# Head of an attention and feed-forward kernel: score tiles cut across pairs, masks of four pairs on TensorE, first up weights in two parts

## The chip, the cores and the metric

The kernel runs on one core of one Trainium2 chip. The metric is the device time of one launch in microseconds (us); where several runs are shown it is their median. The engines are TensorE (PE in the profile, with its weight loads as PEld), ScalarE (ACT), VectorE (DVE), GpSimd (POOL) and SyncE (SP, which here only issues DMAs).

## What is computed

Inputs are q, k, v of 8 sequences, 8 heads, 576 positions and 64 features, 16 further "beacon" keys and values a head that every query may see, and two weights w_in (512 x 2048) and w_out (2048 x 512), all in float32.

```
scores = (q @ concat(beacon_k, k).T) / sqrt(64)       # 576 x 592
scores = where(causal, -1e9, scores)                  # the 16 beacon columns are never masked
a      = softmax(scores)
x      = (a @ concat(beacon_v, v))  -> 4608 tokens x 512
h      = x @ w_in
out    = maximum(0.01 * h, h) @ w_out                 # 4608 x 512
```

## The kernel before

Work goes by pairs of heads: a sequence has four pairs, so there are 32, numbered 0 to 31. For a pair the kernel computes the transposed scores: the 592 keys are cut in five blocks of up to 128, and of each block only the queries that may see it are computed. A score matmul contracts over 64 features, so the two heads of a pair use the upper and the lower 64 rows of TensorE and run side by side, each into a PSUM bank of its own. ScalarE turns a tile of scores into exponentials (scale 0.125) in a bf16 buffer aT, of which there are four. On the diagonal a triangle has to become zero: `triangle` (L287 to L297) does it with a GpSimd affine select on aT, after the exp. `value` (L374) multiplies aT, as weights, with V and a column of ones, whose result is the softmax's denominator; VectorE takes its reciprocal (L388) and scales (L389) into x_nat, and `x_transposes` (L400) turns x_nat into columns of xT on TensorE, with a copy on VectorE or ScalarE (L410).

The feed-forward part works on chunks of 512 tokens. An up (`moe1`, L431) is four 512-column matmuls with w_in (L442) and a leaky relu on ScalarE into gT (L450); there are 16 in a chunk. A down uses gT and w_out: for the first chunk 16 steps of four 512-column matmuls (`moe2_plain`, L507, with its matmul at L512), for the later ones steps of eight 256-column matmuls (L537) that combine sums of operands.

All five engines run their instructions in the order in which the code records them. The first eight pairs (two sequences) are the head, whose order is written out by hand as strings of steps, played by `run` (L692, the strings at L751 to L770): l loads q or k of a pair (L158, issued by GpSimd), V a part of v (L209, L214), i and o a half of w_in (L131) and w_out (L137), q and k turn a loaded operand on TensorE (`t_q`, L231, nine or eighteen small transposes, and a copy at L249), s is a score tile with its exp, m some masks, v half of a pair's values, x its turn into xT, u an up, d a down, w some matmuls on a blank tile whose result nobody reads (`unused`, L653), and W the same in a bank that the next values use (L665). A pair of the head has four score tiles of its own (`score` L256, table SCORES at L50), of 512, 464, 416 and 288 columns in each bank. From pair 8 on, events with due times (L796 to L835) interleave the work, and the scores are cut otherwise: the 1664 columns of a pair lie one after the other (FLAT, L66), pair after pair, and `stretch` (L299) cuts them in tiles of 512, so that a tile may hold the end of one pair and the beginning of the next. Between those events `fill` puts ups and downs on TensorE.

A tile of the framework's pool waits, when it is taken again, for the readers of its last use: score tiles have two such places, all other PSUM tiles of one bank share four. GpSimd's DMAs use eight semaphores in turn, so a DMA is issued only when the one eight before it has landed.

Of the kernel before, what the change touches and what calls it, by code (L numbers as in the profile page):

```python
# [15 lines left out]
def kernel(  # L16
# [33 lines left out]
    SCORES = [  # L50
        [(0, 0, 512, 0)],
        [(1, 112, 464, 512)],
        [(2, 240, 336, 976), (0, 496, 80, 1312)],
        [(3, 368, 208, 1440), (4, 496, 80, 1648)],
    ]
    ACOLS = 1776
    PADS = (1392, 1728)
    BASE = [0, 512, 976, 1440, 1648]
# [3 lines left out]
    LAID = 2 * NPAIR  # L62
    TURNED = 8
    NR = 96

    FLAT = [0, 576, 1040, 1376, 1584, 1664]  # L66

    def acol(g, c, q0):
        if g >= LAID:
            return FLAT[c] + q0 - OFF[c]  # L70
        if c == 0:
            return 1312 if q0 == 496 else q0
        if c == 4:
            return 1648
        return BASE[c] + q0 - OFF[c]

# [12 lines left out]
    blank = singles.tile([128, 128], BF16, name="blank")  # L89
    w_in_sb = [singles.tile([128, NJ, DF // 2], BF16, name=f"w_in_sb{i}") for i in range(2)]  # L90
# [12 lines left out]
    a_bufs = [singles.tile([128, 2, ACOLS], BF16, name=f"aT{i}") for i in range(NA)]  # L103
# [13 lines left out]
    def make_pads():  # L117
        nc.vector.memset(k_all[:, :, NB + S :], 0.0)
        for t in a_bufs:
            for c in PADS:  # L120
                nc.vector.memset(t[:, :, c : c + 48], 0.0)
# [7 lines left out]
    def load_w_in(i):  # L129
        n = DF // 2  # L130
        loaded["w_in", i] = nc.gpsimd.dma_start(  # L131
            out=w_in_sb[i], in_=w_in_r[:, :, i * n : (i + 1) * n]
        )
# [122 lines left out]
    def score(g, n):  # L256
        qT, kT = qk[g]
        if n == 0:
            probs[g] = a_bufs[g % NA]
        aT = probs[g]  # L260
        parts = SCORES[n]
        sc = ps_sc.tile([128, 2, 512], FP32, name="sc", tag="sc")
        c0 = parts[0][3]
        for c, q0, w, col in parts:
            for par in range(2):
                ps_ = slice(par * 64, par * 64 + 64)
                nc.tensor.matmul(  # L267
                    out=sc[:, par, col - c0 : col - c0 + w],
                    lhsT=kT[ps_, c * 128 : (c + 1) * 128],
                    rhs=qT[ps_, q0 : q0 + w],  # L270
# [11 lines left out]
    def mask(g, part):  # L282
        aT = probs[g]
        for lo, n, rows in MASKS[part]:
            triangle(aT, lo, n, rows)
# [582 lines left out]
```

## Time and profile before

| | |
|---|---|
| time, median of 3 runs | 326.24 us (324.75 to 326.97) |
| the profiled execution | 325.23 us, its span 323.5 us, clock of TensorE 0.999 |
| busy: PE, PEld, DVE, ACT, POOL | 98%, 66%, 45%, 62%, 57% of the span |
| score matmuls of the head (L267) into exp (L276) | 32 exps, 25.9 us, 875 ns each on average |
| masks (L289), whole kernel | 160 selects, 59.7 us, 404 ns on average |
| ups (L442) | 640 matmuls, 135.7 us busy |
| w_in's halves: issue to landing | 13.1 + 11.4 us and 19.5 + 11.9 us |

Times in the profile count from the start of the span. Each row of a timeline gives the start, the length, engine and line, the operation, the output and the inputs, the shape, the number of instructions merged in the row, and in brackets how long the engine sat idle before and what ended that. A matmul's length includes the way through the array; the spacing of starts tells what it costs in a row of others.

### The profile page before, as it was taken

What the parts mean: (1) busy time and instruction counts of PE and PEld (TensorE: products, weight loads), DVE (VectorE), ACT (ScalarE), POOL (GpSimd) and SP (SyncE); (2) the same over time, 40 slices, a digit from 0 to 9 for tenths busy, and PEclk for the clock granted to TensorE, in tenths of its full rate; (3) what the DMA queues carried; (4) which work ended last, traced back from release to release, by engine and by line L of the source; (5) the groups of instructions that cost most, each with busy time, mean ns of one, the idle gap of its engine ahead of it and who ended that gap; (6) DMA issues with size and microseconds to landing.
All of it is one profiled execution on the core that took longest, in us unless ns stands there. A gap on an engine that the chain in (4) does not pass through costs nothing.

```text
span 323.5 us, 8521 instructions
## 1 busy us (share of the span) xinstructions
PE 317.3 (98%) x3429; PEld 213.4 (66%) x3429; DVE 146.1 (45%) x297; ACT 199.3 (62%) x336; POOL 184.7 (57%) x354
## 2 busy tenths in 40 slices
PE   8999999999999999999999999999999999999995
PEld 5574565445687558845888888656865785466684
DVE  3473354518446145434552455345444542325444
ACT  4969862487765786478647873786468415653420
POOL 8895968999997687659875977664221000000000
PEclk9999999999999999999999999999999999999999
DMA  8999999999999999999999999999112112000203
GB/s 140 137 206 175 147 214 120 188 165 190 157 138 169 218 147 107 124 174 80 154 192 160 110 127 115 196 128 135 52 53 79 24 54 97 2 1 32 79 20 132
DMA packets 155928, 39.93 MB, mean 123 GB/s; under 512 B 143040, under 2 KB 153152, under 8 KB 155888
## 3 DMA queue, kind: packets, MB, share of 16 engines
q0 software_dynamic: 99824, 18.54, 91.3%
q1 hardware_dynamic: 55792, 20.77, 37.1%
q8 instruction: 27, 0.44, 0.6%
q14 instruction: 13, 0.11, 0.1%
q10 hardware_dynamic: 272, 0.07, 0.1%
HBM read 37.22 MB, written 9.44 MB: 144 GB/s over the span
## 4 chain that ended last, share of the span: by engine, by line
PE 77%; DMA 10%; POOL 5%; ACT 3%; DVE 2%; issue 2%; DVEq 0%; POOLq 0%; ACTq 0%
PE acc L442 31%; PE acc L537 30%; PE av L359 6%; PE sc L314 6%; DMA w_out_sb<-in_moe_w_out_dram 4%; PE acc L512 4%; DMA w_in_sb<-in_moe_w_in_dram 4%; POOL aT L289 2%; DMA gsum<-in_k_dram 2%; ACT aT L333 2%; POOL gsum L158 2%; ACT aT L329 1%; DVE p L565 0%; ACT gT L450 0%; DVE u L565 0%
## 5 line engine op out<-in xcount | busy, mean ns | idle before, releaser
L442 PE MATMUL acc<-xT,w_in_sb 128*128 128x512 bf16 (+1 forms) x640 | 135.7, 358 | 0.3 <-ACT aT L329 0.3
L450 ACT ACTIVATE gT<-acc 128x512 bf16<-128x512 f32 x144 | 82.8, 621 | 46.4 <-PE acc L442 46.2
L442 PEld LDWEIGHTS <-w_in_sb 128*128 128x128 bf16 x640 | 59.6, 98 | 52.4 <-issue 2.9
L289 POOL TENSOR_SCALAR_AFFINE_SELECT aT<-aT 128x256 bf16<-128x256 bf16 (+2 forms) x160 | 59.7, 404 | 51.7 <-ACT aT L329 30.9
L537 PEld LDWEIGHTS <-gT 128*128 128x128 bf16 x512 | 48.8, 98 | 9.1 <-issue 1.8
L333 ACT ACTIVATE aT<-sc 128x1024 bf16<-128x1024 f32 (+3 forms) x64 | 51.8, 895 | 0.0
L537 PE MATMUL acc<-w_out_sb,gT 128*128 128x256 bf16 x384 | 46.2, 273 | 0.4 <-ACT gT L450 0.4
L329 ACT ACTIVATE aT<-sc 128x512 bf16<-128x512 f32 (+3 forms) x64 | 29.0, 522 | 27.9 <-PE sc L314 27.7
L388 DVE RECIPROCAL rec<-av 128x6 f32<-128x6 f32 (+1 forms) x64 | 12.0, 188 | 67.0 <-PE av L359 66.3
L359 PEld LDWEIGHTS <-aT 128*128 128x128 bf16 (+1 forms) x960 | 36.7, 98 | 8.3 <-issue 0.6
L537 PEld LDWEIGHTS <-gsum 128*128 128x128 bf16 x384 | 36.5, 98 | 6.2 <-issue 0.4
L359 PE MATMUL av<-v_aug,aT 128*128 128x65 bf16 (+1 forms) x960 | 39.4, 194 | 0.3 <-ACT gT L450 0.2
L214 POOL DMA_DIRECT2D v_aug<-in_v_dram x40 | 34.2, 859 | 4.1 <-DMA w_in_sb<-in_moe_w_in_dram 3.4
L568 ACT COPY p<-acc 128x512 f32<-128x512 f32 (+1 forms) x25 | 14.5, 580 | 35.6 <-PE acc L537 35.6
L171 POOL DMA_DIRECT2D k_nat<-in_k_dram x48 | 34.9, 733 | 1.3 <-DMA w_out_sb<-in_moe_w_out_dram 0.6
L171 POOL DMA_DIRECT2D q_nat<-in_q_dram x48 | 34.8, 731 | 0.6 <-issue 0.3
L389 DVE TENSOR_TENSOR x_nat<-av,rec 128x384 bf16<-128x384 f32 (+1 forms) x64 | 31.4, 491 | 2.2
L537 PE MATMUL acc<-w_sum,gsum 128*128 128x256 bf16 x256 | 31.9, 273 | 0.0
L276 ACT ACTIVATE aT<-sc 128x1024 bf16<-128x1024 f32 (+3 forms) x32 | 25.9, 875 | 3.5 <-PE sc L267 3.5
L620 DVE TENSOR_TENSOR gsum<-gT 128x1024 bf16<-128x1024 bf16 x16 | 11.0, 688 | 28.1 <-ACT gT L450 28.1
L314 PE MATMUL sc<-qT,kT 64*128 64x80 bf16 (+22 forms) x384 | 22.0, 250 | 0.3
L314 PEld LDWEIGHTS <-kT 64*128 64x128 bf16 x384 | 12.9, 94 | 10.9 <-issue 7.6
(62 smaller groups left out, 227.3 us busy)
## 6 DMA issues: line engine op xcount, KB each, us to landing
out_dram<-p SPq DMA_DIRECT2D x26, 256.0 KB, 3.2
q_nat<-in_q_dram POOLq DMA_DIRECT2D x48, 72.0 KB, 5.5
k_nat<-in_k_dram POOLq DMA_DIRECT2D x48, 72.0 KB, 5.0
v_aug<-in_v_dram POOLq DMA_DIRECT2D x24, 128.0 KB, 6.1
w_in_sb<-in_moe_w_in_dram POOLq DMA_DIRECT2D x2, 1024.0 KB, 11.7
w_out_sb<-in_moe_w_out_dram POOLq DMA_DIRECT2D x2, 1024.0 KB, 11.7
out_dram<-u SPq DMA_DIRECT2D x8, 256.0 KB, 2.7
gsum<-in_q_dram POOLq DMA_DIRECT2D x8, 144.0 KB, 6.9
```

What stands on the lines that cost most here:

```text
L171: nc.gpsimd.dma_start(out=t[:, :, par], in_=(q, k)[which][b, 2 * hp + par].rearrange("(t p) d -> p t d", p=NR),)
L214: nc.gpsimd.dma_start(out=dst[lo : ROWS[c], c, :, 0:D], in_=v[b, :, OFF[c] : OFF[c] + n].rearrange("h p d -> p h d"),)
L276: nc.scalar.activation(out=aT[:, :, c0 : c0 + w], in_=sc[:, :, 0:w], func=AF.Exp, scale=0.125)
L289: nc.gpsimd.affine_select(out=view, in_=view, compare_op=ALU.is_ge, fill=0.0, base=128 - n if lo == 0 else 0, channel_multiplier=-1, patte ...
L314: nc.tensor.matmul(out=(sc[par] if apart else sc[:, par])[:, at : at + b - a], lhsT=kT[ps_, c * 128 : (c + 1) * 128], rhs=qT[ps_, q0 : q0 ...
L329: nc.scalar.activation(out=probs[g][:, par, lo:hi], in_=sc[par][:, at : at + hi - lo], func=AF.Exp, scale=0.125)
L333: nc.scalar.activation(out=probs[g][:, :, lo:hi], in_=sc[:, :, at : at + hi - lo], func=AF.Exp, scale=0.125)
L359: nc.tensor.matmul(out=avv[:, n, 0 : D + 1], lhsT=aT[0 : ROWS[c], par, a0 : a0 + 128], rhs=va[0 : ROWS[c], c, 2 * hp + par, :], start=(c = ...
L389: nc.vector.tensor_tensor(out=x_nat[:, t0:t1].rearrange("p t e d -> p (t e) d"), in0=avv[:, :, 0:D], in1=rec[:, n0:n1, None].to_broadcast( ...
L442: nc.tensor.matmul(out=acc[:, lo:hi], lhsT=w_in_cols(fc, j), rhs=xT[:, j, x0 : x0 + hi - lo], start=(j == 0), stop=(j == NJ - 1), skip_gro ...
L450: nc.scalar.activation(out=gT[i][:, fc, :], in_=acc, func=AF.Prelu, alpha=0.01)
L537: nc.tensor.matmul(out=acc[:, lo : lo + HD], lhsT=left(i, n, fc, tile), rhs=right(n, fc), start=(lo == 0 and fc == 0), stop=(fc == HF - 1) ...
```

## The change

The head now uses the dense cut too. `score`, `mask`, their tables and the second layout of aT are gone; step s takes a tile number from 0 to 25 and calls `stretch`, for the eight pairs' 8 x 1664 columns. For tiles 0 to 12 (pairs 0 to 3) `stretch` is called with `hidden`: after the scores of a tile, `hide` adds a matmul for each piece of a diagonal triangle and each of the two banks, with the identity as weights and a bias tile (0 or -32768, made once by GpSimd) as the moving operand; only the first score matmul of a bank starts it, and the rest add or write. The exp then gives zeros, and those tiles have no masks on GpSimd. Tiles 13 to 25 keep the selects. The first half of w_in is loaded in two parts, both issued before pair 4's q and k; pair 3's q and k are issued before the first V parts; all of pair 5's, pair 6's and most of the second V buffer's loads are recorded ahead of the first matmul. The steps of the head are put in a new order with other numbers of unused matmuls; the first three ups come before pair 4 is turned. The unused steps e and W are gone, and the reciprocals have four buffers instead of two.

```diff
-    def load_w_in(i):
-        n = DF // 2
-        loaded["w_in", i] = nc.gpsimd.dma_start(
-            out=w_in_sb[i], in_=w_in_r[:, :, i * n : (i + 1) * n]
+    def load_w_in(i, part=0, parts=1):
+        n, w = DF // 2, DF // 2 // parts
+        nc.gpsimd.dma_start(
+            out=w_in_sb[i][:, :, part * w : (part + 1) * w],
+            in_=w_in_r[:, :, i * n + part * w : i * n + (part + 1) * w],
         )
...
+    def make_bias():
+        nc.gpsimd.affine_select(
+            out=bias,
+            in_=blank,
+            compare_op=ALU.is_ge,
+            fill=-32768.0,
+            base=0,
+            channel_multiplier=-1,
+            pattern=[[1, 128]],
+        )
...
+    def hide(out, lo):
+        nc.tensor.matmul(
+            out=out,
+            lhsT=ident,
+            rhs=bias[:, lo : lo + out.shape[1]],
+            start=False,
+            stop=True,
+            skip_group_check=True,
+        )
+
-    def stretch(parts, apart=False):
+    def stretch(parts, apart=False, hidden=False):
...
-                        start=True,
+                        start=not hidden or at == 0,
                         stop=True,
                         skip_group_check=True,
                     )
+                end = min(b, FLAT[c] + QT[c][1])
+                if a < end:
+                    hides.append((at, end - a, a - FLAT[c] + (NB if c == 0 else 0)))
                 at += b - a
+        if hidden:
+            for at, n, first in hides:
+                for par in range(2):
+                    hide(bank(par)[:, at : at + n], first)
...
             if op == "s":
-                score(*a)
+                stretch(tile_parts(0, a[0]), hidden=a[0] < 13)
             elif op == "m":
-                mask(*a)
+                triangles(tile_parts(0, a[0]))
...
-        run("l1.1 l2.0 l2.1 V0.0 V0.1 l3.0 l3.1 V0.2 V0.3 V0.4 l4.0 l4.1 i0")
+        make_bias()
+        run("l1.1 l2.0 l2.1 l3.0 l3.1 V0.0 V0.1 V0.2 V0.3 V0.4 i0.0.2 i0.1.2 l4.0 l4.1 l5.0 l5.1 i1 l6.0 l6.1 V1.0 V1.1 V1.2 V1.3")
...
-        unused(13)
+        unused(18)
...
-        run("q0.1 k0 w2.384 s0.0 m0.0 w3.256 s0.1 q1 s0.2 m0.1 k1 s0.3 m0.2")
-        run("w2.384 s1.0 m1.0 q2 s1.1 k2 w2.384 s1.2 m1.1 w2.384 s1.3 m1.2 W0.0.4 s2.0 m2.0 W0.0.4 s2.1 W0.0.6 q3 l5.0 l5.1 s2.2 k3 w4.384 v0.0 m2.1 s2.3 i1 m2.2 W0.1.4 s3.0 m3.0 v1.0 s3.1 v0.1 s3.2 v1.1 m3.1 l6.0 l6.1 s3.3 x0.1 m3.2")
-        run("v2.0 V1.0 V1.1 q4 v2.1 x1 k4.1 v3.0 v3.1 x2.1 s4.0 s4.1 x3 m4.0 V1.2 V1.3 V1.4 l7.0 l7.1 u u s4.2 s4.3 q5 k5 m4.1 m4.2 u o0 u")
+        run("q0.1 k0 w3.384 s0 w1.384 q1 s1 k1 w1.384 s2 q2 s3 k2 w1.384 s4 q3 w1.384 s5 k3 w2.384 s6 w2.384 s7 w2.384 s8 w1.384 v0.0 s9 v1.0 s10 v0.1 s11 v1.1 v2.0 s12 x0 v2.1 x1.1 v3.0 v3.1 x2.1 w3.384 x3.1")
+        run("u u u q4 u k4.1 u s13 m13 V1.4 u s14 l7.0 l7.1 m14 q5 u k5 s15 m15 u s16 m16 o0 u s17 m17 u")
         load_beacon_k(2, B, nc.gpsimd)
-        run("s5.0 s5.1 m5.0 u u u s5.2 s5.3 q6 k6 m5.1 m5.2 o1 u u s6.0 s6.1 m6.0 u v4.0 u v4.1 y4 N8.0 N8.1 u s6.2 s6.3 q7 k7 m6.1 m6.2 u")
+        run("q6 s18 m18 u k6 u s19 m19 o1 u s20 m20 u s21 m21 q7 u k7 v4.0 s22 m22 u N8.0 N8.1 v4.1 y4")
...
-        run("u v5.0 u v5.1 N9.0 s7.0 s7.1 m7.0 d x5 v6.0 v6.1 T8 d s7.2 s7.3")
+        run("s23 m23 v5.0 s24 m24 N9.0 v5.1 s25 m25 v6.0 d x5 v6.1 d T8")
...
-        run("m7.1 m7.2 N9.1 u b8.2 b9.2 b10.2 b11.2 x6 v7.0 T9 v7.1 d d d N10.0 N10.1 d V2.0 V2.1 x7 t0 T10")
+        run("v7.0 N9.1 d b8.2 b9.2 b10.2 b11.2 x6 v7.1 T9 d d d N10.0 N10.1 d V2.0 V2.1 x7 t0 T10 d d d d")
```

## The prediction, made before the result was known

> **What bounds the kernel now.** I read the page first: busy shares, then the 40 slices. TensorE (PE) is busy 98% of the span and 9 tenths in every slice but the two ends, with its full clock granted.
>
> ```profile
> span 323.5 us, 8521 instructions
> PE 317.3 (98%) x3429; PEld 213.4 (66%) x3429; DVE 146.1 (45%) x297; ACT 199.3 (62%) x336; POOL 184.7 (57%) x354
> PE   8999999999999999999999999999999999999995
> ```
>
> So the question for any edit is how much it adds to or takes from what TensorE issues, and which of its waits it ends. The table of stretches (columns: stretch, length, busy time of PE, PEld, DVE, ACT, POOL, then clock and DMA) says that after the head (from 76.9 us) there is almost nothing left to win by waiting less:
>
> ```profile
> 5.60:25.20 19.60, 19.27 (x398) 12.69 (x396) 11.99 (x27) 15.23 (x21) 18.45 (x38) 1.00 1.70 174
> 76.90:200.00 123.10, 122.74 (x1405) 89.84 (x1404) 56.85 (x118) 85.15 (x151) 96.80 (x182) 1.00 1.75 147
> ```
>
> The first stretch looks as full but is not all work: it holds warm-up matmuls (L657, L669). Next the timeline of TensorE at a place where warm-ups (L657, 128 rows) and score matmuls (L267, 64 rows, two at a time) alternate:
>
> ```profile
> 11.58 0.50 PE L657 MATMUL av<-blank 128*128 128x384 bf16 x2
> 12.01 0.35 PE L267 MATMUL sc<-qT,kT 64*128 64x336 bf16 x4
> 12.29 0.50 PE L657 MATMUL av<-blank 128*128 128x384 bf16 x2
> 12.73 0.30 PE L267 MATMUL sc<-qT,kT 64*128 64x208 bf16 x4
> ```
>
> Two 384-column matmuls stream for 2 x 0.163 = 0.33 us (the group of four at 15.73 takes 0.82, its last matmul 0.33: 0.163 apart), yet the scores start 0.43 and 0.44 us after them: 0.10 us is lost at the change of row shape. Then what ends the head's first part, on ScalarE, GpSimd and TensorE:
>
> ```profile
> 17.20 3.89 ACT L276 ACTIVATE aT<-sc 128x576 bf16<-128x576 f32 x5 [0.84 <-PE sc L267]
> ...
> 20.24 1.73 POOL L289 TENSOR_SCALAR_AFFINE_SELECT aT<-aT 128x256 bf16<-128x256 bf16 x5
> 21.93 0.59 POOL L158 DMA_DIRECT2D gsum<-in_q_dram  x1
> 22.51 0.61 POOL L158 DMA_DIRECT2D gsum<-in_k_dram  x1
> 23.12 0.70 POOL L289 TENSOR_SCALAR_AFFINE_SELECT aT<-aT 128x256 bf16<-128x256 bf16 x2
> ...
> 22.78 1.49 PE L359 MATMUL av<-v_aug,aT 128*128 128x65 bf16 x30
> 24.11 0.42 PE L405 MATMUL tp<-ident,x_nat 112*128 112x112 bf16 x5
> 24.46 0.59 PE L267 MATMUL sc<-qT,kT 64*128 64x512 bf16 x4
> 24.98 0.43 PE L405 MATMUL tp<-ident,x_nat 112*128 112x112 bf16 x5
> 25.25 1.52 PE L442 MATMUL acc<-xT,w_in_sb 128*128 128x512 bf16 x6
> ...
> 52.24 3.61 PE L512 MATMUL acc<-w_out_sb,gT 128*128 128x512 bf16 x16 [0.34 <-DMA w_out_sb<-in_moe_w_out_dram]
> ```
>
> The last exp of pair 3 ends at 21.09 (17.20 + 3.89), its last two masks wait behind two DMA issues until 23.82, pair 3's value matmuls take 1.33 us instead of the 0.95 of an undisturbed x30, and the first up matmul (L442) starts at 25.25. Later one wait of the head, for the second half of w_out at 52.2, shows on TensorE.
>
> **What the Trainium skill says.** TensorEngine Tiling (Array Packing), Key Properties: "Mode switching requires drain". The 0.10 us above is that; the trace agrees and prices it. TensorE: Matmul & The Clock Gate, "Wait — 56ns, not 53.3ns?": warm matmuls of 128 columns start 55.6 ns apart. The trace agrees: the five transposes from 24.98 to 25.25 move 576 columns in 0.27 us. The same page, "Architectural detail": GpSimd's queue is in order, so masks wait behind DMA issues, as at 21.93. PSUM — Partial Sum Buffer, The four PSUM rules: a matmul without the first flag adds where an earlier one wrote since the bank was cleared, and overwrites elsewhere. So the mask matmuls need no help from another engine; nothing in this trace shows such an addition at these tiles.
>
> **The change, part by part.**
> Mask matmuls: a pair's triangles are 112 + 3 x 128 + 80 = 576 columns, in two banks, so twice the five transposes: 0.54 us a pair, 2.1 us for four, in 46 pieces. Bounds: 46 x 0.033 us (a small value matmul) = 1.5, and 46 x 0.1 (a weight load's duration, should it not overlap) = 4.6. I take 2.1.
> Row-shape changes: counted in the issue order of the two built programs, 116 before and 133 after. Pairs 4 to 7 had their score tiles two by two (8 groups); now 13 tiles stand alone between ups, and the turns of pair 4 stand between ups too. 17 x 0.095 = +1.6 us (0.09 to 0.11 each: 1.5 to 1.9).
> Score pieces: 512 matmuls for 480, in pairs, with 1% fewer columns: +0.06. Exps: 16 instructions per four pairs as before, 1% fewer elements: 0.1 less on ScalarE.
> Warm-ups: after the first transposes 12 of 384 columns, 3 of 256 and 18 of 112 (1.95 + 0.33 + 0.90) become 17 of 384 (2.76): -0.4. Five more ahead of them fall into the wait for the first q.
> Masks taken off GpSimd: 20 x 0.36 us there, hidden but for pair 3's: 1.33 - 0.95 = 0.4 of TensorE.
> Other waits that can go: w_out's at 52.2 (0.34 idle, 0.5 between the starts), because the downs come later, and some 0.4 on exps and copies between 7 and 14 us. New: the first up on its last copy, 0.2 to 0.3 (the copy, L410, takes 0.64 and three quarters of an up 0.65, less its start). Net with the masks' 0.4: -1.1 (0 to -2.9; 2.9 is all that the starts between 5.6 and 76.9 show beyond columns and shape changes).
> DMAs moved: q and k of pair 3 ahead of five V parts, pair 4's behind w_in's first half. The queue's data order is what counts: the third V part, first needed as a set, lands as before (8.16 + 8.4 = 16.5). w_in's first half landed at 24.5 (13.07 + 11.4); without pair 4's two loads before it (landing 1.4 apart from the V before them) I estimate 23.1, its first part 21. Ups need them at about 24.7 and 29. Pair 4's q and k, some 24.5, are needed after three ups, 27.7. Cover of 1 to 3 us each; once gone, lateness counts in full. w_in's second half still lands near 31.4, for the ninth up at 35. The bias select (0.32) delays only issues of a DMA queue that already has a backlog. GpSimd's first mask of pair 4 stands ahead of the last V part, which waits as now for w_in (3.4 idle); the masks behind it serve value matmuls near 44 us.
> Sum: 2.1 + 1.6 + 0.1 - 0.4 - 1.1 = **+2.2 us** (rounded), as TensorE has no other slack to put it in.
>
> Cross-check by the path. The first exp starts 0.25 later (one shape change, two mask matmuls, a part of a warm-up). A dense exp then takes 0.94 (two are 1.87). TensorE's part of a tile is 0.22 scores, 0.19 for two shape changes and 0.1 to 0.3 masks; where a q or k turn (0.29 and up to 0.19 of changes) and a warm-up join, it is 1.1 and more, so for six to seven tiles TensorE sets the pace, at 0.15 to 0.2 each. The last exp ends near 22.4 instead of 21.1. Then the values of pair 3 (0.95 and 0.2 latency), DVE's two steps (0.65), the turn (0.27) and gaps: first up at 24.75, its last quarter 0.27 late: effectively 25.0, 0.25 ahead of now. But now, pair 4's turns (2 x 0.29), two score tiles (24.46 to 24.98) and some four changes are done by then: 1.45 us, so +1.2. In pairs 4 to 7, seven to eight more groups at 0.19: +1.4. Less 0.5 for w_out: +2.1.
>
> The sum is against the profiled execution, 325.23 us (the span of 323.5 and 1.7 around it), which would become 327.4; the median of the three runs, 326.24, is 1.0 above that execution, so the forecast for the median is 326.24 + 2.2 = **328.4**.
>
> **The rivals.**
> Faster: the head of TensorE is slack in disguise. With no masks on GpSimd the exps would run unbroken from 7.7 for 12.7 us, to 20.4; 2.3 us later the first up starts, 22.7, with weights there at 21 (now 24.5, which would be the gate): -2.3 + 0.3 for its last copy + 1.45 of moved work - 0.5 for w_out, and the changes of pairs 4 to 7 hidden in waits for exps = -1.1, 325.1. For it: 6 us of warm-ups and waits before 25 us, the 0.84 gap on ScalarE. Against it: 17 warm-ups stay, and pairs 4 to 7 show no waits to hide in. It decides where pair 3's last exp ends before 21.
> Slower: TensorE, in order, stops at pair 0's first values, which wait for V, with the score tiles queued behind. If pair 3's loads delay the third V part by their own 1.5 us, ScalarE runs dry and all that follows is late: +2.2 + 1.5 = +3.7, and 329.9. It decides where those values start after 17.5. Against it: in both orders the same loads precede that part.
> No effect: the parts cancel (changes cheaper, all waits gone): 326.2. And the two-part weights do nothing in the forecast, because pair 3's turn, not the weights, gates the first up.
>
> **How the numbers follow.** Forecast 0.62, faster 0.18, slower 0.14, no effect 0.06. The forecast's own range is +0.4 (all 2.9 of waits gone) to +3.6. About 1% (3.3 us) is what a measurement tells from no change. Below 323.0 lies the end of the faster case, 0.05. Above 329.5 lie most of the slower case and the forecast's upper end: 0.20. Leaving 0.1 on each side: 325.0 to 330.2.
>
> **What would show it.** Right: 46 mask matmuls at 35 to 60 ns between starts; 0.1 us at each shape change; pair 3's last exp after 22; first up near 24.7 with w_in long there; no wait for w_out; all later stretches as now. Wrong: first up before 23.5, or score groups without the 0.1 us, or a TensorE wait of over a microsecond on V, q or k.

## The result and the profile after

The changed kernel takes 330.48 us, median of 6 runs (329.73 to 331.05); six runs of the kernel before beside them took 326.43 us (324.75 to 330.89). The ratio is 1.0134 (95% interval 1.0105 to 1.0162): it is 1.3% slower, some 4.1 us by the medians. Ratios, here and below, leave out slow executions, those more than 1.5% above the fastest of their kernel, such as the 330.89. The profiled executions lie further apart, 330.61 against 325.23 us, because that of before was one of its shorter ones and that of after is at its median. The forecast was 328.4.

In the changed kernel the mask matmul is L262, the score matmul L287, the exp L313, the select on GpSimd L251, the value matmul L337, the unused matmul L627, the turn of q or k L236, the up L412, the first chunk's down L482, natural loads L164, parts of v L207. The page's first lines answer to those of before:

```profile
span 328.9 us, 8624 instructions
...
PE 322.0 (98%) x3496; PEld 215.7 (66%) x3496; DVE 144.5 (44%) x292; ACT 199.9 (61%) x337; POOL 179.8 (55%) x336
```

TensorE is as full as before, over a span 5.4 us longer. The stretches (length, busy time of PE, PEld, DVE, ACT, POOL, then clock, DMA share and GB/s) show where it is no longer full: the head's first part has no idle time left (0.33 us before), the later one has 1.51 us in 125 where 0.36 in 123.1 was:

```profile
5.60:25.30 19.70, 19.70 (x409) 13.68 (x408) 11.78 (x26) 15.07 (x19) 12.71 (x20) 1.00 1.75 175
80.00:205.00 125.00, 123.49 (x1442) 90.62 (x1440) 57.80 (x121) 86.40 (x153) 98.88 (x183) 1.00 1.78 142
```

TensorE's timeline in the kernel before, at the first turn of q and at the values of a later pair:

```profile
4.32 1.43 PE L657 MATMUL av<-blank 128*128 128x128 bf16 x13
5.67 0.47 PE L243 MATMUL tp<-ident,gsum 64*64 64x64 bf16 x18
...
99.43 0.72 PE L359 MATMUL av<-v_aug,aT 128*128 128x65 bf16 x18
```

The same places in the changed kernel, and those that the forecast named:

```profile
4.31 2.10 PE L627 MATMUL av<-blank 128*128 128x128 bf16 x18
6.34 0.47 PE L236 MATMUL tp<-ident,gsum 64*64 64x64 bf16 x18
...
18.31 0.46 PE L262 MATMUL sc<-bias,ident 128*128 128x128 bf16 x6
18.61 0.53 PE L337 MATMUL av<-v_aug,aT 128*128 128x65 bf16 x12
...
25.34 2.99 PE L412 MATMUL acc<-xT,w_in_sb 128*128 128x512 bf16 x12
...
54.26 0.42 PE L337 MATMUL av<-v_aug,aT 128*128 128x65 bf16 x8
55.16 0.30 PE L337 MATMUL av<-v_aug,aT 128*128 128x65 bf16 x4 [0.49 <-POOL aT L251]
...
82.89 0.83 PE L287 MATMUL sc<-qT,kT 64*128 64x96 bf16 x15 [0.43 <-DVE x_nat L359]
...
103.80 0.53 PE L337 MATMUL av<-v_aug,aT 128*128 128x65 bf16 x12
105.15 0.35 PE L337 MATMUL av<-v_aug,aT 80*128 80x65 bf16 x6 [0.82 <-DMA v_aug<-in_v_dram]
```

Six mask matmuls take 0.30 us from the first to the next group, 0.05 each, as forecast. But the first turn of q starts at 6.34 us instead of 5.67, behind 18 unused matmuls of 0.107 us each; pair 7's values stop for a mask; and far behind the head two more stops come: at 83 us scores wait for VectorE's x_nat (0.43 idle), and at 104 us the eighteen value matmuls that go through in one row before are split, as the last six wait for v, by 0.98 us more than their usual spacing (0.82 idle).

All of TensorE's spacings, start to start, added up by parts give the account of the two profiled executions. "Columns" is what the matmuls take at the undisturbed spacing of their shape (0.216 us for 512 columns, 0.056 for 128); "changes" is what is lost beyond that where the row or column shape changes; "stops" is spacing of over 0.06 us beyond it elsewhere. The number of changes is in brackets.

| part of TensorE's time (us) | before | after | difference |
|---|---|---|---|
| start to first turn of q | 5.67 | 6.34 | +0.67 |
| turn of q to first up | 19.58 | 19.00 | -0.58 |
| ... columns | 13.50 | 14.34 | +0.84 |
| ... changes | 4.70 (43) | 3.67 (38) | -1.03 |
| ... stops and rest | 1.38 | 0.99 | -0.39 |
| first up to pair 7's turn | 30.67 | 35.33 | +4.66 |
| ... columns | 27.54 | 29.33 | +1.79 |
| ... changes | 1.70 (18) | 3.80 (40) | +2.10 |
| ... stops | 0.78 | 1.16 | +0.38 |
| ... rest | 0.65 | 1.04 | +0.39 |
| one more down done by then | | | -0.86 |
| pair 7's turn to the last matmul, same work | | | +1.46 |
| sum (last matmul's start) | 319.93 | 325.28 | +5.35 |

"Pair 7's turn" is here the turn of its values into xT (x7). Columns come to +1.8 in all (0.84 + 1.79 - 0.86): the mask matmuls' 2.1 less unused ones. Changes come to +1.1. The rest, 2.5, is the later start, new stops in the head, and what comes after it.

### The profile page after: what moved, and what is told of

Read it like the earlier page. It is cut to its first block, busy times and chain, and to the rows that moved or that the text cites. A ratio compares the mean times of both kernels' runs of the same rounds, so it can differ in the third digit from the quotient of the medians.

```text
span 328.9 us, 8624 instructions
## 1 busy us (share of the span) xinstructions
PE 322.0 (98%) x3496; PEld 215.7 (66%) x3496; DVE 144.5 (44%) x292; ACT 199.9 (61%) x337; POOL 179.8 (55%) x336
## 4 chain that ended last, share of the span: by engine, by line
PE 84%; ACT 6%; DMA 3%; POOL 2%; issue 1%; DVE 1%; DVEq 0%; ACTq 0%; SPq 0%; POOLq 0%
PE acc L412 33%; PE acc L507 27%; PE sc L287 8%; PE av L337 7%; PE acc L482 4%; ACT aT L313 3%; PE av L627 3%; DMA v_aug<-in_v_dram 2%; PE tp L236 2%; ACT gT L420 2%; ACT aT L309 1%; PE sc L262 1%; DMA kT<-k_nat 1%; POOL q_nat L164 1%; POOL aT L251 1%
## 5 line engine op out<-in xcount | busy, mean ns | idle before, releaser
L412 PE MATMUL acc<-xT,w_in_sb 128*128 128x512 bf16 (+1 forms) x640 | 136.0, 358 | 0.1
L412 PEld LDWEIGHTS <-w_in_sb 128*128 128x128 bf16 x640 | 59.2, 98 | 52.2 <-issue 2.8
L251 POOL TENSOR_SCALAR_AFFINE_SELECT aT<-aT 128x256 bf16<-128x256 bf16 (+2 forms) x140 | 53.2, 404 | 63.7 <-ACT aT L309 30.9
L313 ACT ACTIVATE aT<-sc 128x1024 bf16<-128x1024 f32 (+3 forms) x96 | 78.4, 887 | 4.2 <-PE sc L262 2.4
L337 PEld LDWEIGHTS <-aT 128*128 128x128 bf16 (+1 forms) x960 | 36.5, 98 | 8.4 <-issue 1.4
L337 PE MATMUL av<-v_aug,aT 128*128 128x65 bf16 (+1 forms) x960 | 39.4, 194 | 1.3 <-DMA v_aug<-in_v_dram 0.8
L164 POOL DMA_DIRECT2D q_nat<-in_q_dram x48 | 34.8, 729 | 0.2
L164 POOL DMA_DIRECT2D k_nat<-in_k_dram x48 | 34.8, 728 | 0.3
L207 POOL DMA_DIRECT2D v_aug<-in_v_dram x40 | 33.9, 856 | 0.1
L287 PE MATMUL sc<-qT,kT 64*128 64x80 bf16 (+22 forms) x512 | 33.1, 251 | 0.7 <-DVE x_nat L359 0.4
L287 PEld LDWEIGHTS <-kT 64*128 64x128 bf16 x512 | 17.0, 94 | 16.8 <-issue 11.2
L535 DVE TENSOR_TENSOR p<-acc,p 128x512 f32<-128x512 f32 (+1 forms) x17 | 11.1, 659 | 13.5 <-PE acc L507 13.1
```

The lines of the kernel that those rows point to most:

```text
L164: nc.gpsimd.dma_start(out=t[:, :, par], in_=(q, k)[which][b, 2 * hp + par].rearrange("(t p) d -> p t d", p=NR),)
L207: nc.gpsimd.dma_start(out=dst[lo : ROWS[c], c, :, 0:D], in_=v[b, :, OFF[c] : OFF[c] + n].rearrange("h p d -> p h d"),)
L251: nc.gpsimd.affine_select(out=view, in_=view, compare_op=ALU.is_ge, fill=0.0, base=128 - n if lo == 0 else 0, channel_multiplier=-1, patte ...
L287: nc.tensor.matmul(out=bank(par)[:, at : at + b - a], lhsT=kT[ps_, c * 128 : (c + 1) * 128], rhs=qT[ps_, q0 : q0 + b - a], start=not hidde ...
L313: nc.scalar.activation(out=probs[g][:, :, lo:hi], in_=sc[:, :, at : at + hi - lo], func=AF.Exp, scale=0.125)
L337: nc.tensor.matmul(out=avv[:, n, 0 : D + 1], lhsT=aT[0 : ROWS[c], par, a0 : a0 + 128], rhs=va[0 : ROWS[c], c, 2 * hp + par, :], start=(c = ...
```

## The experiments

Times are medians, with the ratio to runs of the kernel before that were made beside them. Those runs' medians lay between 326.09 and 326.85 us from group to group, and the changed kernel itself was measured in one group only, so a difference of less than about 0.7 us between a median here and its 330.48 is not clear of noise; in such cases the argument rests on the profiles. Positions come from one profiled execution each. "First up" is the start of the first w_in matmul: 25.25 us before, 25.34 after.

**The unused matmuls at the start.**

```diff
-        unused(18)
+        unused(13)
```

> The changed kernel with 13 unused 128-column matmuls ahead of the first turn of q instead of 18. Theory A (the head is a sum of what TensorE issues, and the five extra ones do not fit into the wait for the first q): the first turn of q starts at 5.67 us as before the change instead of 6.34, all that follows is 0.67 us earlier, time against the changed kernel -0.5 to -0.7 us. Rival B (the exps set the head): the first exp starts 0.6 earlier, but pair 3's last exp, and so the first up, by less than 0.3. Rival C (the five keep the clock up): the turn starts at 5.67 but the matmuls behind it run slower, no gain.

Measured: 330.75 us, ratio 1.0118 (1.0087 to 1.0148). The turn of q starts at 5.81, 0.53 earlier, the first up at 24.99, 0.35 earlier than in the changed kernel, and the later stops of the head, up to that for x_nat, are 0.35 to 0.36 earlier too. The last matmul starts at 325.23, 0.05 earlier. Between the two lies the stop for v:

```profile
105.09 0.35 PE L337 MATMUL av<-v_aug,aT 80*128 80x65 bf16 x6 [1.13 <-DMA v_aug<-in_v_dram]
```

The values start at the same time as after, with 1.13 us idle for 0.82. So the extra matmuls do delay the head (theory A, at half its size), but this stop swallows the gain: in this profile the arrival of v decides when the program ends.

**No mask matmuls.**

```diff
-                stretch(tile_parts(0, a[0]), hidden=a[0] < 13)
+                stretch(tile_parts(0, a[0]), hidden=False)
```

> The changed kernel without its 46 mask matmuls; pairs 0 to 3 are then not masked at all, on any engine. Theory A: -2.1 us of issue, and 5 row-shape changes fewer (128 for 133), -0.5: the time falls by 2.0 to 2.8 us. Rival B (the exps set the pace, mask matmuls lie beside them): the first up moves by under 0.5 us and the time by under 0.6. Rival D (weight loads between the small matmuls are not hidden): it falls by 4 to 5.

Measured: 327.62 us, ratio 1.0039 (1.0021 to 1.0057). First up at 23.41, 1.93 earlier; last matmul 322.66, 2.62 earlier, because the stop for v is gone as well (that part of v landed at 102.5, after 5.8 us on its way instead of 6.5). Theory A holds in mechanism, and its size is met at the first up; the time fell by 2.9 us, since the stop for v went too. And with no masks in four pairs at all, the changed order is still slower than the kernel before: 0.2 to 0.6%.

**Score tiles two by two.**

```diff
-"... u s13 m13 V1.4 u s14 l7.0 l7.1 m14 q5 u k5 s15 m15 u s16 m16 o0 u s17 m17 u"
+"... u s13 s14 m13 V1.4 u l7.0 l7.1 m14 q5 u k5 s15 s16 m15 m16 u o0 u s17 s18 m17 m18 u"
```

and likewise s19 with s20 and s23 with s24.

> The changed kernel with score tiles 13 to 24 (pairs 4 to 7) two by two where their operands allow it (five twos), the same ups and downs around them; 124 row-shape changes for 133. Theory A: 9 x 0.095 = -0.85 us, all of it between 25 and 60 us. Rival B (the changes lie in waits for exps there, or two tiles at once make the second wait for its exp and the matmuls behind it for a score buffer): no gain, -0.2 to +0.5, with new waits on exps.

Measured: 330.98 us, ratio 1.0125 (1.0097 to 1.0153). Changes between the first up and pair 7's turn fall from 40 to 31 and their cost from 3.80 to 2.95 us: 0.094 each, as theory A says. The stretch is 35.31 us long, as before this edit (35.33): its stops rose from 1.16 to 2.09. TensorE's timeline of this kernel, where the second tile of a two reads keys just turned:

```profile
35.37 0.34 PE L287 MATMUL sc<-qT,kT 64*128 64x384 bf16 x2 [0.45 <-DVE kT L242]
```

Rival B is right on the time, with another wait than it named.

**The same with room behind the key turns.**

```diff
-"... q5 u k5 s15 m15 u s16 m16 o0 u s17 m17 u"
+"... q5 u k5 u s15 s16 m15 m16 u o0 s17 s18 m17 m18 u"
...
-"... u s21 m21 q7 u k7 v4.0 s22 m22 u N8.0 N8.1 v4.1 y4"
+"... u q7 u k7 u s21 s22 m21 m22 v4.0 u N8.0 N8.1 v4.1 y4"
```

> The changed kernel with score tiles 13 to 24 two by two again, now with at least one up between the turn of a pair's keys and the first score tile that reads them; 8 row-shape changes fewer. Theory A (a change costs 0.095 us on TensorE, and in the first attempt the gain went into stops for keys just turned): -0.75 us against the changed kernel, the stretch between the first up and pair 7's turn 0.6 to 0.9 shorter than its 35.3 us. Rival B (two tiles at once always make something else late: an exp, a score buffer, a mask): that stretch within 0.3 of 35.3.

Measured: 330.30 us, ratio 1.0132 (1.0112 to 1.0151); the stretch is 35.38 us. Some matmul records are missing from this trace, so its changes are not counted. The stop has moved once more, to the exp that frees the score buffer, and pair 7's values wait 0.76 instead of 0.49 for their mask:

```profile
37.13 0.39 PE L287 MATMUL sc<-qT,kT 64*128 64x192 bf16 x4
38.11 0.40 PE L287 MATMUL sc<-qT,kT 64*128 64x144 bf16 x6 [0.59 <-ACT aT L313]
...
55.44 0.30 PE L337 MATMUL av<-v_aug,aT 128*128 128x65 bf16 x4 [0.76 <-POOL aT L251]
```

So by the spacings the changes cost what was forecast, but single tiles among the ups also give the exps and copies time; taking the changes away in these two ways gave no time. No edit won this part of the loss back.

**No unused matmuls behind the first turn of q.**

```diff
-"q0.1 k0 w3.384 s0 w1.384 q1 s1 k1 w1.384 s2 q2 ..."
+"q0.1 k0 s0 q1 s1 k1 s2 q2 ..."
```

> The changed kernel without the 17 unused matmuls of 384 columns between the first turn of q and pair 3's last turn (2.76 us of issue, 5 row-shape changes of 133 go with them). Theory A (TensorE's pace sets pair 3's last exp): first up 1.5 to 3 us earlier, time -1.5 to -2.8. Rival B (the exps set the pace: 12.7 us unbroken from 8.3): pair 3's last exp ends at 21 to 21.5 instead of 23.4, first up 2 earlier, but the gaps turn into waits, -1 to -2. Rival C (without them the granted clock falls and the head's matmuls run at half speed): time +0.5 to +3, visible in the clock of the slices of the head.

Measured: 329.53 us, ratio 1.0088 (1.0061 to 1.0115). In the profiled execution (330.90) the first up is at 25.93, 0.6 later than in the changed kernel. Up to 14 us the forecast's faster rival comes true, as ScalarE's timeline shows: the seven exps of the first six tiles (the one at a pair's end is cut in two) without a gap, 1.0 us a tile. Then TensorE stops twice, 0.68 us at 14.0 and 0.63 at 15.6, the second time for an exp, and the table of stretches (after the busy times of the five engines the granted clock, DMA share and GB/s) shows the clock at 0.51 and 0.81 behind that:

```profile
8.23 5.97 ACT L313 ACTIVATE aT<-sc 128x1024 bf16<-128x1024 f32 x7 [0.69 <-PE sc L262]
15.13 2.92 ACT L313 ACTIVATE aT<-sc 128x512 bf16<-128x512 f32 x4 [0.92 <-PE sc L262]
```

```profile
13.80:16.70 2.90, 1.59 (x20) 0.87 (x19) 0.55 (x1) 1.98 (x4) 0.61 (x2) 1.00 1.97 161
16.70:19.00 2.30, 2.30 (x37) 2.02 (x37) 0.75 (x2) 1.58 (x3) 1.95 (x3) 0.51 1.25 209
19.00:22.00 3.00, 3.00 (x67) 2.23 (x65) 1.41 (x5) 2.48 (x4) 0.59 (x1) 0.81 1.22 203
```

At that clock 2.3 x 0.49 + 3.0 x 0.19 = 1.7 us of work is lost. The seven executions at a clock of 0.998 and more took 328.4 to 329.7, some 1 to 2 us less than the changed kernel; three, this one among them, at 0.995, lost it again. Rivals B and C are both at work. None of the changed kernel's six executions lost its clock, so what the unused matmuls seem to buy is the clock in those three of ten; that the two stops brought it down is read from the order of events in this one profile, and was not tested.

**No four downs at the end of the head.**

```diff
-"... V2.0 V2.1 x7 t0 T10 d d d d"
+"... V2.0 V2.1 x7 t0 T10"
```

> The changed kernel without the four downs that it has at the end of the head, ahead of the first stretch of pair 8; the same downs then fall among the later steps, so that loads of v which are placed by the count of steps are issued earlier against TensorE's work. Theory A (the 0.98 us stop for v at 105 us comes from those four downs: v's last part of the batch was issued at 98.6 us, 7.4 later than before the change, with values only some 4.6 later): that part is issued about 2 to 4 us earlier against its values, the stop is gone, time -0.8 to -1.0 us against the changed kernel. Rival B (the queue that carries v is full there, and v lands when it lands): it still lands near 105, no gain.

Measured: 330.04 us, ratio 1.0126 (1.0099 to 1.0154). In the profile (329.17, its quickest execution) the stop for v is gone and the last matmul starts 1.44 us earlier, 0.2 of which is the head's; the stop for x_nat at 83 us is gone too. But 0.31 us idle for keys turned by DMA (at 80.7) and 0.47 for a gT (at 90.7) have come, and the median gained only 0.4, which is not clear of noise: between theory A and B. (Its turn of q started at 5.68, though it too has 18 unused matmuls: full speed came at 4.6 us in this execution.)

**Three edits at once**: that one, 13 unused matmuls, and pair 9's natural load behind pair 7's masks.

```diff
-"... v5.0 s24 m24 N9.0 v5.1 s25 m25 v6.0 ..."
+"... v5.0 s24 m24 v5.1 s25 m25 N9.0 v6.0 ..."
...
```

> The changed kernel with three edits: no four downs at the end of the head, 13 unused 128-column matmuls at the start for 18, and pair 9's first natural load (two DMA issues, 1.45 us of GpSimd) recorded behind the masks of pair 7's last tile. Theory A (behind the stop for v nothing absorbs the gains of the head): the sum of -0.95 (v), -0.35 (as the first up moved with 13) and -0.65 (pair 7's values no longer wait for masks), -1.7 to -2.0 us against the changed kernel, about 328.6. Rival B (another wait takes the place of each): -1 or less.

Measured: 332.01 us, ratio 1.0171 (1.0129 to 1.0213), slower than the changed kernel by the median; its six executions lie in two groups, two at 329.4 and 329.6 and four at 331.8 to 333.2. The profiled one (331.81) is of the second group. The stop for pair 7's mask is gone, but in TensorE's timeline the keys that pass by that load, a DMA transpose and those behind it come late:

```profile
74.71 0.72 PE L287 MATMUL sc<-qT,kT 64*128 64x256 bf16 x10 [0.73 <-POOL kT L222]
...
83.31 0.67 PE L287 MATMUL sc<-qT,kT 64*128 64x128 bf16 x10 [2.25 <-DMA kT<-k_nat]
```

Rival B, and more than it. GpSimd issues each of these DMAs in 0.72 us and is busy without a gap from 48.3 to 60.9 us, so what is put ahead there pushes something else back. The two quick executions have no trace; that they escaped these stops is likely, not shown.

**The loads of v alone**, 0.6 pairs earlier among the later steps:

```diff
-... ((-0.1, 0.1)[n > 3] if b == 2 else 0.3 * n - 0.4) ...
+... ((-0.1, 0.1)[n > 3] if b == 2 else 0.3 * n - 1.0) ...
```

> The changed kernel with its later loads of v (from the fourth batch element's on, and the third's last) placed 0.6 pairs earlier among the steps, the four downs at the end of the head kept. Theory A (the stop for v at 105 us is the place of these loads against the steps): the fifth part of the batch's v is issued some 4 us earlier against its values, no stop for v, no other new stop over 0.3 us, time -0.8 to -1.0 against the changed kernel. Rival B (as without the four downs: these queues carry the transposed keys too, which then come late): a stop for k of 0.3 us or more, gain under 0.6.

Measured: 329.69 us (329.32 to 329.99), ratio 1.0099 (1.0069 to 1.0128): 0.8 below the changed kernel. GpSimd issues the fifth part at 95.25 instead of 98.59. TensorE's timeline:

```profile
102.71 0.53 PE L337 MATMUL av<-v_aug,aT 128*128 128x65 bf16 x12
103.08 1.04 PE L507 MATMUL acc<-w_sum,gsum 128*128 128x256 bf16 x8
103.95 0.72 PE L337 MATMUL av<-v_aug,aT 128*128 128x65 bf16 x18
```

The eighteen value matmuls, the last six of which need that part, start 0.87 us after the eight matmuls ahead of them, which is their own time (8 x 0.109), and go through in one row; no new stop has come. The head is 0.2 later here, the last matmul 0.81 earlier: 1.0 us, theory A. The stop for x_nat stayed. In the kernel before that part was issued at 91.23 and landed at 97.8; its values started at 99.43, and at 103.80 after: the change moved the load by 7.4 us and its values by 4.4.

**The four downs in the kernel before.**

```diff
-"... V2.0 V2.1 x7 t0 T10"
+"... V2.0 V2.1 x7 t0 T10 d d d d"
```

> The kernel before with the four extra downs at the end of the head alone. Theory A (they shift the loads placed by step counts against TensorE's work): a new stop of TensorE of 0.3 to 1.2 us for v or k between 60 and 110 us, time +0.3 to +1.0. Rival B (the stop in the changed kernel comes from its later head): no stop, within 0.3.

Measured: 326.96 us, ratio 1.0011 (0.9987 to 1.0036), no change that this interval (-0.4 to +1.2 us) shows; theory A's +0.3 to +1.0 lies in it. There is no stop for v or k, but four idle times of 0.23 to 0.45 us, three for x_nat and one for xT's DMA. So the downs alone do not make the stop for v: it needs the changed kernel's later loads too. Which part of its new order does that was not tried.

**w_in in two parts alone**, in the kernel before:

```diff
-        run("... V0.4 l4.0 l4.1 i0")
+        run("... V0.4 i0.0.2 i0.1.2 l4.0 l4.1")
```

> The kernel before, with one part of the change alone: w_in's first half in two parts, both ahead of pair 4's q and k. Theory A (pair 3's turn gates the first up, and the loads have cover): 0 within 0.3 us of the kernel before; first part landed near 21, second near 23, first up still near 25.2. Rival B (the first up waits for w_in in the kernel before): first up and all behind it 0.3 to 1 us earlier. Rival C (pair 4's loads, later by the weights, stop their turn): +0.3 to +1, with a stop for q or k between 25 and 28 us.

Measured: 327.69 us, ratio 1.0048 (1.0025 to 1.0071): slower, against all three expectations. In the profiled execution, which was one of its longer ones (329.56), the cause is none of the loads named:

```profile
6.33 0.69 PE L244 MATMUL tp<-ident,gsum 64*64 64x64 bf16 x18 [0.45 <-DMA gsum<-in_q_dram]
...
16.39 0.82 PE L658 MATMUL av<-blank 128*128 128x384 bf16 x2
...
20.91 0.47 PE L244 MATMUL tp<-ident,gsum 64*64 64x64 bf16 x18
```

A turn takes 0.69 us until 20 us, and 0.47 from then on; two unused matmuls of 384 columns take 0.82 where 0.50 is usual. The Trainium skill (TensorE: Matmul & The Clock Gate, Part 1) has this: TensorE starts at half its clock, and a window of some 3.4 us of activity releases it, wherever the window happens to lie; 128 columns then take 56 ns instead of 107. The 18 at 0.107 us above agree. Here the release came only at 20 us, 19 us after the first matmul at 1.07, so such a window of activity was not enough in this execution, and the profile's own clock column shows 1.00 throughout: this half speed is read from the spacings alone. From the first values on, the path to the first up is as long as in the kernel before (8.5 us for 8.9), so the weights' two parts cost nothing there. In 12 of its 19 executions the mean granted clock was 0.995 or less, in 1 of 37 of the kernel before beside them. Of the other seven, five took 326.4 to 326.9 us, like the kernel before. So the loss goes mostly with TensorE's clock; why this edit should touch it was not found.

**Mask matmuls alone**, in the kernel before's own tiles:

```diff
-                    start=True,
+                    start=g >= NPAIR or col == c0,
...
+        if g < NPAIR:
+            for c, q0, w, col in parts:
+                if q0 == OFF[c]:
+                    for par in range(2):
+                        hide(sc[:, par, col - c0 : col - c0 + QT[c][1]], 16 if c == 0 else 0)
```

and no m0 to m3 in the head's steps.

> The kernel before, with one part of the change alone: the masks of the first four pairs added by matmuls (40 of them) in its own score tiles, no GpSimd masks there. Theory A (TensorE's issue): +2.0 for the matmuls and 5 row-shape changes more, +0.5, less the 0.4 that pair 3's values waited for masks: +1.8 to +2.4 us against the kernel before; that is half of the change's loss. Rival B (the exps set the pace of the head, the matmuls lie beside them): under +0.6.

Measured: 327.95 us, ratio 1.0044 (1.0019 to 1.0070): +1.4 us, 0.6 to 2.3. Its profiled execution too ran at half speed, until 10 us, so its first up (28.88) is no measure; from there to the first up it took 18.8 us where the kernel before took 17.2 between the same turns, +1.65. By the medians about a third of the change's loss comes from this part; by the interval it may be a seventh or the half that was forecast.

**18 unused matmuls alone**, in the kernel before:

```diff
-        unused(13)
+        unused(18)
```

> The kernel before with one part of the change alone: 18 unused 128-column matmuls ahead of the first turn of q for 13. In the profiles so far TensorE's matmuls went over from half speed to full speed at different times: 4.4, 4.6, 5.5, 5.9, 6.3, 6.9 us, and in two kernels with 13 of them not before 10 and 20 us. Theory D (half speed lasts on where TensorE pauses before the switch; the extra five bridge that): the first turn of q starts near 6.3 in a profile and at full speed, single times lie closer together than those of the kernel before (324.9 to 328.4), lowest 0.3 to 0.6 us higher, median 0.3 to 0.8 us lower. Theory A (only issue counts): all times +0.35 to +0.6.

Measured: 326.71 us (324.38 to 329.37), ratio 1.0004 (0.9976 to 1.0033): no change within an interval of -0.8 to +1.1 us, which also holds theory A's +0.35 to +0.6, and times as far apart as those of the kernel before. In its profile full speed came at 4.7 us and q landed at 6.20, so the turn waited 0.59 us for q and the five cost nothing. Whether they cost 0.67 or nothing thus depends on two things that vary from launch to launch. Theory D's promise for the times did not come true; what spreads the times of the kernel before stays open.

**That, and pair 3's masks ahead of pair 6's loads.**

```diff
-"... m3.1 l6.0 l6.1 s3.3 x0.1 m3.2"
+"... m3.1 s3.3 x0.1 m3.2 l6.0 l6.1"
```

> The kernel before with 18 unused matmuls and with the loads of pair 6's q and k recorded behind pair 3's last masks on GpSimd. Theory A: pair 3's values no longer wait for masks, first up 0.3 to 0.4 us earlier than with 18 alone, time -0.3. Rival B (something else ends last there: the first up waits for w_in, or pair 3's turn for VectorE): under 0.1.

Measured: 326.43 us, ratio 0.9999 (0.9978 to 1.0020). The values of pair 3 no longer wait, but the first up does, 0.22 us idle, for w_in: rival B. (Stops of 0.29 us for v at 19 us and of 1.46 us for keys turned by DMA at 61 us came in this profile too.) But w_in landed late here, at 25.82 (24.48 in the profile of the kernel before), and with 18 alone pair 3's values took only 0.94 us, so there was nothing to win there. This pair of profiles doesn't tell whether the 0.4 us can be had in the kernel before.

**Dense tiles with their masks on GpSimd**, loads between them as in the kernel before:

```diff
-"... s6 w2.384 s7 w2.384 s8 w1.384 v0.0 s9 ... s12 x0 ..."
+"... s6 m6 l5.0 l5.1 w2.384 s7 m7 w2.384 s8 m8 i1 w1.384 v0.0 s9 m9 ... s12 m12 l6.0 l6.1 x0 ..."
...
```

and `hidden=False` for all tiles.

> The changed kernel with the masks of its first four pairs on GpSimd again, tile by tile, and the loads of pairs 5 and 6, of w_in's second half and of the second v recorded between them as in the kernel before. Theory A (mask matmuls cost their issue and 5 row-shape changes, 2.6 us; pair 3's last two masks cost up to 0.7 in its values): -1.6 to -2.6 us against the changed kernel, about 328.3; what is left to the kernel before is dense tiles, single tiles among the ups, and the later stops. Rival B (masks on GpSimd make the values of pairs 0 to 3 wait, as GpSimd also issues loads): -1 or less.

Measured: 329.98 us, ratio 1.0107 (1.0060 to 1.0154). First up at 23.66, but the turn of q was 0.77 earlier (5.57), as full speed came at 3.9 us in this execution; from turn to first up it took 18.09 us: 0.91 less than the changed kernel and 1.02 more than with no masks at all. By the spacings, its values stop seven times for 1.31 us together, most of it for masks. So the matmuls cost 1.93 and save about 1.0 of such stops: 0.9 net. Theory A had the parts right, and took the masks on GpSimd for cheaper than they are. The stop for v has grown to 1.17 us idle, and swallowed part of this gain too.

**That, with v's loads earlier** (the two edits together).

> The changed kernel with the masks of its first four pairs on GpSimd and with the later loads of v 0.6 pairs earlier. Theory A (the stop for v swallowed what the first of these gave; without it both count): first up near 23.7, no stop for v, time the sum of 1.7 (first up) and 1.0 (the stop) below the changed kernel, about 327.9, and the last matmul 2.4 to 2.9 us earlier in the profile. What is left to the kernel before, some 2 us, is then the row-shape changes and new stops between the first up and pair 7's turn. Rival B (keys transposed by DMA come late once the head is shorter): a stop for k of over 0.3 us, gain 1.5 or less.

Measured: 328.96 us, ratio 1.0089 (1.0058 to 1.0119), 1.5 below the changed kernel; in the profiles the last matmul starts 1.90 earlier. No stop for v, none for k over 0.24. The first up came at 24.33, with a turn of q at 6.06. Of the 0.8 that is missing from 2.7, 0.5 is the later turn of q (6.06 for 5.57 in the run above), 0.2 the way from there to the first up. What is left against the kernel before is 2.9 us; from the first up to pair 7's turn TensorE takes 35.4 us as in the changed kernel, with its 40 changes and 0.57 us idle for pair 7's masks.

**Unused matmuls on 64 rows**, in the kernel before, and everything together in the changed one:

```diff
-                lhsT=blank,
+                lhsT=blank[0:64],
...
```

> The kernel before with its unused matmuls behind the first turn of q on 64 rows instead of 128, so that they have the row shape of the scores beside them; 12 row-shape changes fewer, all ahead of the first up. Theory A (TensorE's issue sets the head's first part, a change costs 0.095): first up 0.7 to 1.1 us earlier, time -0.6 to -1.1 against the kernel before. Rival B (exps or w_in set the first up): first up within 0.3, with a stop for an exp or w_in. Rival C (half of the rows is not enough to keep the clock up): matmuls of the head longer or a granted clock under 1.0, time +0.5 or more.

> The changed kernel with all that the runs suggest: masks of the first four pairs on GpSimd, score tiles of pairs 4 to 7 two by two, unused matmuls of the head on 64 rows, no four downs at the end of the head; 111 row-shape changes, where the kernel before has 115 and the changed one 132. Theory A (the loss is the sum of mask matmuls, changes and late stops): within 0.7 us of the kernel before (0.4 of changes less, 0.1 of columns less, pair 3's masks and pair 7's waits as cost). Rival B (dense tiles cost in themselves, for example by exps of 1024 columns that come late): 1.5 us or more above the kernel before.

Measured: 326.97 us, ratio 1.0040 (1.0011 to 1.0068), and 333.57 us, ratio 1.0196 (1.0146 to 1.0247). The first gains nothing even at full clock (lowest 326.16, of the kernel before 325.27), though 12 changes less should have given 1.1 us; no trace shows that case. In its profiled execution, and in three more of its 15, the clock fell: the row of the page, in 40 slices, is

```profile
PEclk9759999999999999999999999999999999999999
```

Rival C: it is 0.7 and 0.5 in the slices from 8 to 25 us. The second kernel's six executions took 330.1 and 330.3, and 333.3 to 335.1; the profiled one (333.90) stops for 2.91 us at 84 us for keys turned by DMA, as in the run of three edits, with a clock of 0.7 in the slice there; so it can't tell whether dense tiles cost in themselves. Rival B's time came, but not by its reason.

No version beat the kernel before. The three that equal it within their intervals are its own order, with 18 unused matmuls (two of them) or with the four downs at the end of the head.

## Why the prediction was wrong

The direction was right and the size was half: +2.2 forecast, +4.1 by the medians, +5.35 between the profiled executions.

*Right.* TensorE's issue sets the time. The forecast's terms add up to +2.3, not the +2.2 that it carries on, which changes nothing; and the row of 1.87 us that it reads as two dense exps holds one of 1024 and one of 928 elements (full ones start 0.90 to 0.92 apart). Mask matmuls: 2.1 forecast, 1.93 to the first up when they are taken out, and +1.8 of columns with the unused ones counted, as in the sum. Changes: 17 x 0.095 forecast; in the head's main part 22 more cost 2.10, 0.095 each, and in the first part five fewer and 0.5 us of old waits at them took 1.03 off. V's third part landed at 15.6, w_in's parts at 20.9 and 23.2, pair 4's q and k at 23.8 and 24.5: all ahead of their use, and w_out's wait is gone. The path's "first up at 24.75, its last quarter 0.27 late" came at 25.34 and 0.24 late: 0.59 behind the forecast, less than the 0.67 that the start alone was behind. Pair 3's last exp ended at 23.42 for 22.4.

*The step "all later stretches as now"* failed first: 1.46 us were lost behind the head. 0.98 of it is one stop for v. The forecast treated the work from pair 8 on as fixed, but its loads are placed by counting ups and downs, so a head with other counts, and later loads of its own, moves them against the values: 7.4 us for 4.4. Moving those loads alone brought 1.0 us in the profile and 0.8 in the median. This stop also hid what other edits gave, which is why 0.35 us from the start showed in no time. The largest other new stop is the one for x_nat at 83 us, 0.43 us idle. It stands in all nine profiles of the changed kernel with its four downs at the end of the head, in none of the three without them, and three of its kind came into the kernel before with those downs. In part it takes the place of two stops of 0.27 and 0.16 us (for an exp and for a gT) that the profile of the kernel before has and that of the changed one hasn't.

*The step "Five more ahead of them fall into the wait for the first q"* failed: cost 0 forecast, +0.67 in the profile, 0.35 of it confirmed by going back to 13. I had taken the wait for q as cover without asking whether this execution had one: 13 matmuls from 4.32 at 0.107 us each end about when q lands, 5.50, so five more stand in full (0.54). The other 0.13 is half speed, which lasted to 5.4 us in that execution and to 6.3 in the changed kernel's. In other executions the cover was there: with 18 in the kernel before, 0.59 us of waiting for q were left, and without the last downs the changed kernel's turn started at 5.68. So this term depends on the launch.

*The term "net -1.1" for waits* was mis-sized by about 0.9: measured some -0.2. The waits that the change ends were counted (w_out 0.5, old waits in the first part), those it makes were not, except the last copy's: 0.65 between pair 7's value matmuls, and some 0.27 for pair 7's keys at 46.5 (read from the spacing alone), 0.9 together. The sentence "the masks behind it serve value matmuls near 44 us" looked only at pair 4's masks. GpSimd's timeline of the changed kernel, where pair 7's stand:

```profile
52.43 0.52 POOL L181 CAST bk<-bk_raw 128x384 bf16<-128x384 f32 x1
52.89 0.41 POOL L251 TENSOR_SCALAR_AFFINE_SELECT aT<-aT 128x256 bf16<-128x256 bf16 x1
53.24 1.45 POOL L164 DMA_DIRECT2D q_nat<-in_q_dram  x2
54.69 1.05 POOL L251 TENSOR_SCALAR_AFFINE_SELECT aT<-aT 128x256 bf16<-128x256 bf16 x3
```

Pair 7's last tile was scored at 50.5, its masks come at 54.69, behind two loads, with values due at 54.5. The 0.4 for pair 3's masks did come: their value matmuls take 0.93 us in the changed kernel, for 1.33.

*The step to the median* erred the other way: I took the kernel after to lie as far above its profiled execution as the one before (1.0 us). It lay 0.1 below. 3.15 us too little between the profiles, less this 1.1, is the 2.1 by which the forecast missed.

The rivals. Faster needed exps without gaps: that came up to 14 us only once the unused matmuls were gone, and then, in three executions of ten, the clock went. Slower named V's third part: pair 0's values did start at 17.52, just beyond its limit of 17.5, but that part had landed at 15.56; the time near its 329.9 came by other ways. That the two-part weights do nothing holds for the first up; alone, in the kernel before, they came out 0.5% slower, together with a lower clock, which nothing in my list covers.

Open stay the cause of that clock, part of the other half microsecond behind the head, and whether dense tiles cost in themselves. Two ways of saving the changes' cost at the single tiles were tried, and neither made the kernel faster.

## What to carry to other kernels

On a full engine the added instructions can be priced from the trace to one or two tenths of a microsecond, though taking them away again need not bring the time back; what misses is the waits, and the new ones have to be looked for as hard as those that go. Follow every queue that the edit fills to its last reader, and where later work is placed by counts, check its loads against the new counts far beyond the place of the edit. Look for the stop that ends last before judging an edit by its time: a gain of 0.35 us ahead of a load that arrives late shows nowhere.

## What the runs showed of the hardware

Two things slow TensorE's matmuls in the head, and only one shows in the profile's clock column. Half speed at the start ended between 3.9 and 7 us in seventeen of nineteen profiles, and at 10 and 20 us in two, with the column at 1.00. The granted clock, which the column does show, fell to 0.51 after two stops of 0.6 to 0.7 us where unused matmuls had been taken out, and to 0.7 and 0.5 where they used 64 of the 128 rows, though TensorE was busy for 7.75 of 8.2 us and all of 8.2 in those slices.
